# Attention and gated convolution: the attention output of 13 of 16 quads of heads is turned by transposing transfers, and all work is put in a new order

## The chip, the cores and the metric

The kernel runs on one core of a Trainium2 chip. The metric is the device time of one execution in microseconds. Before the change three runs took 176.99, 177.25 and 177.54 us, the median being 177.25 us. The profile shows one further execution, of 176.23 us.

## The reference, cut to what matters

The inputs q, k and v have 8 batches, 8 heads, 576 positions and 64 elements a head. All is float32 in memory and float16 on the matmul engine.

```python
scores = q @ k.T / sqrt(64)                  # for each batch and head, 576 x 576
mask   = (pos_i // 64) >= (pos_j // 64)      # causal in blocks of 64 positions
x      = softmax(where(mask, scores, -1e9)) @ v
x      = x.transpose(0, 2, 1, 3).reshape(8, 576, 512)   # heads side by side
gate   = sigmoid(sum_k conv_w[k] * x[:, t - 4 + k])     # causal, 5 taps a feature
out    = (gate * (x @ w_val)) @ w_out
```

The attention leaves a tile of x with positions on the partitions. The gate's convolution over time and the product with `w_val` both need features on the partitions and positions along the row. So every tile of x is turned once, and the change is about who turns it.

## The kernel before

**Units.** A pair p (0 to 31) is two heads of batch p // 4. A quad Q (0 to 15) is two pairs. A stage n from 0 to 7 is the gated part of batch n on its first 512 positions; the last 64 positions of four batches each are collected in stages 8 and 9.

**One quad.** SyncE loads q and k of four heads (`Lq`, `Lk`, 576 KB each) and v (`Lv`, `Lvt`). VectorE, GpSimd or ScalarE casts them (`cq`, `ck`, `cv`, `cvt`), and VectorE turns q and k (`dq`, `dk`, line 202). TensorE makes the scores in three pieces and a last one (`s.Q.0` to `s.Q.2`, `sl`), ScalarE the exponentials (`e`, `el`, line 242), GpSimd zeroes what the mask hides (`m`), TensorE multiplies with v (`av`, 35 matmuls a head), VectorE divides by the sums (`n`, lines 289 and 290) and writes the tile `x16[p % 4]`, 128 positions x 5 blocks x 128 features of two heads in float16.

**The turn, before.** For every quad TensorE transposes the five 128 x 128 blocks of each of its two pairs against an identity into PSUM (`xtr`, line 298, 10 matmuls a quad). VectorE, for the last two quads ScalarE, copies the two pairs into `xts[b % 2]` (`xt`, line 156). There are two such buffers, one batch each. `xe` copies the last 64 positions aside (`xtl`).

(Each pair has two heads of 64 features, so one block of it has 128 features and the five blocks hold 640 positions, of which 576 are real. A quad's `xtr` covers both pairs: 2 x 5 blocks, and each block is one matmul with its weight load. The profile counts 160 of them for 16 quads.)

**One stage.** TensorE runs the convolution as 80 small matmuls on all of the batch's rows (`cn`, slices of 32 x 32 with the taps on diagonals), ScalarE the tanh (`th`), TensorE `x @ w_val` in four pieces (`val`), VectorE gate times value (`gv`, line 347), TensorE the product with `w_out` in four pieces (`o`), VectorE or ScalarE copies them out of PSUM (`oc`), SyncE stores (`st`, lines 378, 382, 376).

**What sets the order.** One string of words, `PLAN`, is read from left to right; each word issues one of the operations above on the engine behind its `@` (A ScalarE, D VectorE, P GpSimd, S SyncE's queue; a digit is the PSUM bank of a TensorE operation). Each engine runs its own words strictly in that order, and semaphores between engines follow from the data. `w.512` is a matmul on zeros whose result nobody reads. A DMA is issued by SyncE's queue in its place in the string and waits there for its buffer or its data, so all DMAs behind it wait too.

```python
def xtrans(p, cnt, m):                       # before: line 294
    for e in range(2):
        for i in range(5):
            nc.tensor.transpose(out=f16(bk(m, e))[:, 128 * i:128 * i + 128],
                                in_=x16[(p + e) % NX16][0:128, i, 0:2, 0:64], ...)
```

Of the kernel before, what the change touches and what calls it, by code (L numbers as in the profile page):

```python
# [11 lines left out]
wz@D pk@D pp.2@P Lq.0@S Lk.0@A Lk.1@S Lq.1@S cq.0@D dq.0@D id Lcw@S ck.0@D dk.0@D ck.1@P dk.1@D  # L12
w.512@0 w.512@0 w.512@0 w.512@0 w.512@0 w.512@0 w.512@0 w.512@0 w.512@0 w.512@0 w.512@0 w.512@0
w.512@0 w.512@0 w.512@0 s.0.2@02 s.0.1@46 tb cq.1@P fo@D Lv.0.0@S e.0.2@A dq.1@D e.1.2@A p4.0@P
cwc@P s.0.0@02 pv.1@P Lq.2@S e.1.1@A px.0@P cw@6 cT@D Lv.0.3@S cq.2@D e.0.1@A pp.0@P Lv.0.1@S pv.0@P
e.1.0@A w.512@7 w.512@7 sl.0@64 Lvt.0@S el.0.1@A pp.1@P s.1.2@24 cvt.0@D cv.0.3@D el.0.0@A e.0.0@A
e.3.2@A Lv.0.2@S cv.0.2@D s.1.0@60 Lk.2@S cv.0.1@P e.3.0@A dq.2@D e.2.0@A Lwv.1@S Lq.3@S p4.1@P
m.1@P cv.0.0@P av.1@4 m.0@P pp.3@P e.2.2@A s.1.1@06 n.1@D e.2.1@A e.3.1@A Lwv.0@S ck.2@P pp.4@P
av.0@4 dk.2@D s.2.0@02 n.0@D m.2@P av.2@6 m.3@P Lv.1.0@S cq.3@P e.4.0@A DG@D e.5.0@A av.3@4 s.2.2@02
wv.1@A n.2@D wv.0@A xtr.0.2@6 n.3@D e.5.2@A xtr.2.2@4 Lk.3@S e.4.2@A Lk.4@S xt.0.2@D ck.3@P s.2.1@26  # L20
e.4.1@A xt.2.2@D xe.0@P wv.2@P ck.4@P wv.3@D Lv.1.3@S e.5.1@A cn.0@04 m.5@P dk.3@D dq.3@D Lv.1.2@S
Lv.1.1@S th.0.0@A val.0.0@2 cv.1.2@P gv.0.0@D Lvt.1@S val.0.1@3 th.0.1@A Lq.4@S s.3.2@06 Lwo.0@S
val.0.3@2 e.7.2@A gv.0.1@D sl.1@46 dk.4@D gv.0.3@D Lq.5@S cv.1.1@P e.6.2@A cv.1.3@D Lwo.3@S
val.0.2@3 Lvt.2@S gv.0.2@D el.1.0@A cq.4@D px.1@P pp.5@P s.3.0@04 cvt.1@P el.1.1@A e.6.0@A e.7.0@A
Lwo.1@S dq.4@D cv.1.0@P av.5@6 s.3.1@20 n.5@D m.4@P av.4@4 Lv.2.0@S cq.5@D e.7.1@A Lk.5@S e.6.1@A
m.7@P n.4@D m.6@P s.4.0@06 av.7@2 av.6@4 e.8.0@A ck.5@P n.7@D n.6@D e.9.0@A Lk.6@S s.4.1@06 e.8.1@A
Lwo.2@S Lv.2.2@S wo.1@P xtr.4.2@2 Lv.2.3@S Lq.6@S xt.4.2@D wo.0@P e.9.1@A xtr.6.2@4 s.4.2@02 e.8.2@A
xt.6.2@D e.9.2@A m.9@P dq.5@D Lv.2.1@S cn.1@46 val.1.0@0 th.1.0@A dk.5@D xe.1@P gv.1.0@D Lq.7@S
ck.6@P val.1.1@1 s.5.0@24 cq.6@P th.1.1@A e.11.0@A e.10.0@A gv.1.1@D o.0.1@0 oc.0.1@D o.0.2@1
oc.0.2@D cv.2.3@D sl.2@46 el.2.0@A el.2.1@A val.1.2@0 Lvt.3@S cv.2.2@P Lq.8@S s.5.1@24 Lk.7@S  # L30
cvt.2@P Lv.3.2@S e.11.1@A val.1.3@1 m.8@P gv.1.2@D o.0.3@0 dq.6@D dk.6@D s.5.2@46 e.10.1@A cv.2.1@P
Lv.3.3@S e.11.2@A e.10.2@A cv.2.0@P av.8@2 gv.1.3@D n.8@D o.0.0@1 av.9@6 m.11@P s.6.0@24 oc.0.3@D
oc.0.0@A n.9@D av.11@0 st.0.0@S m.10@P cq.8@A e.13.0@A av.10@6 e.12.0@A cq.7@P n.11@D o.1.1@4
cvt.3@P oc.1.1@A n.10@D s.6.1@02 e.13.1@A Lv.3.1@S xtr.8.2@6 xtr.10.2@4 xt.8.2@D Lv.3.0@S xt.10.2@D
e.12.1@A s.6.2@26 dq.7@D cn.2@04 e.12.2@A ck.7@P dk.7@D xe.2@D cv.3.3@P Lk.8@S cv.3.0@P e.13.2@A
m.13@P th.2.0@A o.1.3@2 oc.1.3@D m.12@P dq.8@D th.2.1@A o.1.0@3 sl.3@06 cv.3.1@P el.3.1@A val.2.3@2
cv.3.2@P gv.2.3@D s.7.0@46 oc.1.0@A val.2.2@3 Lvt.4@S Lv.4.3@S o.1.2@2 ck.8@P el.3.0@A e.15.0@A
e.14.0@A gv.2.2@D s.7.2@06 val.2.1@3 e.14.2@A dk.8@D Lq.9@S e.15.2@A Lq.10@S oc.1.2@D Lk.9@S
Lv.4.0@S av.12@4 gv.2.1@D s.7.1@02 n.12@D e.14.1@A Lv.4.1@S val.2.0@6 Lv.4.2@S gv.2.0@D av.13@4
st.0.1@S e.15.1@A s.8.0@06 m.14@P m.15@P av.14@2 n.13@D av.15@4 st.1.0@S ck.9@P Lv.5.3@S e.16.0@A  # L40
e.17.0@A n.14@D n.15@D o.2.1@0 oc.2.1@D Lv.5.2@S s.8.2@26 Lk.10@S e.16.2@A xtr.14.2@4 xtr.12.2@0
Lk.11@S xt.14.2@D e.17.2@A cq.10@P o.2.0@2 oc.2.0@A s.8.1@46 xt.12.2@D e.16.1@A e.17.1@A cn.3@02
cq.9@P cv.4.3@D val.3.1@4 val.3.2@5 Lvt.5@S dk.9@D xe.3@P Lv.5.1@S dq.9@D th.3.0@A gv.3.1@D th.3.1@A
s.9.0@06 e.18.0@A gv.3.2@D val.3.0@4 gv.3.0@D cvt.5@D e.19.0@A o.2.2@5 Lq.11@S oc.2.2@D sl.4@02
cv.4.0@P dq.10@D o.2.3@4 el.4.0@A cvt.4@P cv.4.1@P Lv.6.3@S s.9.1@06 el.4.1@A e.18.1@A oc.2.3@D
m.16@P Lk.12@S cv.4.2@P st.1.1@S e.19.1@A ck.10@D av.16@2 n.16@D cn.8@40 val.8.0@6 th.8.1@A th.8.0@A
# [24 lines left out]
gv.7.1@D val.9.0@1 val.7.3@5 cn.9@26 th.9.0@A gv.9.0@D val.9.1@0 th.9.1@A val.7.2@2 gv.9.1@D
oc.6.0@A val.7.0@1 gv.7.2@D o.9.0@0 o.9.1@4 gv.7.0@D st.6.1@S gv.7.3@D oc.9.1@A st.6.0@S o.7.0@1
oc.9.0@D o.7.1@0 o.7.2@2 oc.7.0@A o.7.3@1 oc.7.1@D st.9.0@S st.7.0@S oc.7.2@D oc.7.3@AD st.7.1@SA
# [4 lines left out]
def kernel(  # L78
# [12 lines left out]
    fp16 = mybir.dt.float16  # L91
# [3 lines left out]
    B, H, SEQ, D = q.shape  # L95
# [14 lines left out]
    def ring(n, shape, dt, tag):  # L110
        return [const(shape, dt, f"{tag}_{i}") for i in range(n)]
# [23 lines left out]
    xts = ring(NX, [128, 4, 644], fp16, "xt")  # L135
# [8 lines left out]
    slot = {}  # L144
# [4 lines left out]
    def two(s):  # L149
        return PS[0:128, s:s + 2]  # L150

    def f16(ap):
        return ap.bitcast(fp16)

    def copy(eng, o, i):
        (eng.copy if eng is nc.scalar else eng.tensor_copy)(out=o, in_=i)  # L156
# [279 lines left out]
    def pads_x(i, m):  # L436
        m.memset(xts[i][0:128, 0:4, 0:4], 0.0)
# [47 lines left out]
```

## Time and profile before

| what | value |
|---|---|
| median of three runs | 177.25 us |
| the profiled execution | 176.23 us, of which the span of the engines is 174.4 us |
| mean granted TensorE clock | 0.971 of full speed |
| TensorE busy | 161.7 us, 93% of the span |
| VectorE, ScalarE, GpSimd busy | 129.9, 131.5, 69.2 us |
| first convolution matmul, last matmul of all | starts at 28.41 us, ends at about 170.15 us |
| moved by DMA | 40.30 MB, mean 231 GB/s |

The span runs from the first instruction to the last event of the core; 1.83 us of the execution lie outside it. Three stretches have different limits: the head up to the first convolution (loads, casts, the first exponentials), the long middle, and the 4.25 us behind the last matmul (copy out, store, its landing). The page gives shares for the whole span, so the stretches have to be asked for one by one.

### The profile page before, as it was taken

Reading aid. Unit: us, or ns where it says so; the run is one execution under the profiler, and the core shown is the slowest. Engines: PE = TensorE matmul, PEld = TensorE weight load, DVE = VectorE, ACT = ScalarE, POOL = GpSimd, SP = SyncE. Lnnn points to the kernel's source line nnn. Section 1 sums busy time; section 2 is a strip of 40 time slices with the busy share of each in tenths; the row PEclk is TensorE's granted clock in tenths of the full one; section 3 lists DMA queues with packets and bytes.
Section 4 is the critical chain, followed back from the end, with each engine's and each line's share of the span. In section 5 each row is a group of like instructions: output and inputs, shape, how many; then the busy total and the mean of one; then the engine's idle time right before and its main releaser. Section 6 shows DMA issues by size and latency. Waiting matters only on the chain.

```text
span 174.4 us, 6916 instructions
## 1 busy us (share of the span) xinstructions
PE 161.7 (93%) x3013; PEld 94.8 (54%) x3013; DVE 129.9 (74%) x202; ACT 131.5 (75%) x160; POOL 69.2 (40%) x141
## 2 busy tenths in 40 slices
PE   7448999989999999999999999999999999999990
PEld 2123677367445673576366854675437563855640
DVE  1599399998878887879697798779899836741650
ACT  3039999987969899767979799899879698456320
POOL 1284565954595817085505134433603022210000
PEclk9985599999999999999999999999999999999999
DMA  5999997999799699999997596999320005403246
GB/s 176 397 323 296 381 327 195 312 264 301 194 336 271 187 325 334 277 296 319 343 337 242 114 402 198 305 233 357 136 79 2 4 4 194 172 4 120 81 163 241
DMA packets 48216, 40.30 MB, mean 231 GB/s; under 512 B 38453, under 2 KB 38453, under 8 KB 48186
## 3 DMA queue, kind: packets, MB, share of 16 engines
q1 hardware_dynamic: 47898, 39.01, 72.8%
q10 hardware_dynamic: 288, 0.85, 1.4%
q8 instruction: 23, 0.38, 0.9%
q14 instruction: 7, 0.06, 0.1%
HBM read 30.42 MB, written 9.44 MB: 228 GB/s over the span
## 4 chain that ended last, share of the span: by engine, by line
PE 70%; DVE 12%; ACT 7%; issue 5%; DMA 3%; ACTq 0%; DVEq 0%
PE PS L99 65%; ACT pt L242 6%; PE PS L298 5%; DMA qks<-in_q_dram 3%; DVE x L290 3%; DVE qk L156 2%; DVE kT L202 2%; DVE gv L347 2%; DVE qT L202 1%; DVE osb L156 1%; DVE rc L289 1%; ACT osb L156 1%; DVE xt L156 0%; DVE v16t L156 0%; ACT v L156 0%
## 5 line engine op out<-in xcount | busy, mean ns | idle before, releaser
L242 ACT ACTIVATE pt<-PS 128x1024 f16<-128x1024 f32 (+1 forms) x112 | 97.8, 937 | 23.3 <-PE PS L99 20.9
L99 PE MATMUL PS<-qT,kT 32*128 32x64 f16 (+4 forms) x768 | 37.6, 291 | 5.7 <-DVE kT L202 4.5
L99 PEld LDWEIGHTS <-pt 128*128 128x128 f16 x960 | 32.0, 99 | 7.1 <-issue 3.1
L99 PE MATMUL PS<-w_out,gv 128*128 128x512 f16 x144 | 35.3, 380 | 0.1
L347 DVE SCALAR_TENSOR_TENSOR gv<-th,PS 128x512 f16<-128x512 f32 x36 | 24.0, 681 | 14.6 <-ACT th L332 9.3
L156 POOL CAST qk<-qks 128x1152 f16<-128x1152 f32 x22 | 25.3, 1165 | 21.4 <-DVE kT L202 12.3
L99 PE MATMUL PS<-v,pt 128*128 128x65 f16 x896 | 33.0, 195 | 0.9 <-ACT pt L242 0.7
L99 PE MATMUL PS<-xt,w_val 128*128 128x512 f16 x128 | 31.9, 381 | 0.0
L99 PEld LDWEIGHTS <-kT 32*128 32x128 f16 x768 | 16.2, 95 | 28.2 <-issue 16.7
L263 POOL MEMSET pt<- 64x384 f16 x32 | 13.8, 430 | 37.8 <-ACT pt L242 37.1
L290 DVE TENSOR_TENSOR x<-PS,rc 128x640 f16<-128x640 f32 x32 | 26.4, 824 | 1.1
L99 PEld LDWEIGHTS <-w_val 128*128 128x128 f16 x160 | 13.7, 98 | 14.6 <-issue 3.8
L99 PEld LDWEIGHTS <-gv 128*128 128x128 f16 x144 | 12.8, 98 | 14.4 <-issue 0.9
L202 DVE STREAM_TRANSPOSE qT<-qk 128x576 f32<-128x576 f32 x16 | 19.9, 1243 | 0.1
L202 DVE STREAM_TRANSPOSE kT<-qk 128x576 f32<-128x576 f32 x16 | 19.7, 1243 | 0.0
L332 ACT ACTIVATE th<-PS 128x1024 f32<-128x1024 f32 (+1 forms) x20 | 17.7, 947 | 2.2 <-PE PS L99 2.2
L156 DVE COPY osb<-PS 128x512 f32<-128x512 f32 (+1 forms) x20 | 13.4, 671 | 7.3 <-PE PS L99 5.8
L156 ACT COPY osb<-PS 128x512 f32<-128x512 f32 (+1 forms) x17 | 9.7, 583 | 9.0 <-PE PS L99 8.3
L289 DVE RECIPROCAL rc<-PS 128x10 f32<-128x10 f32 x32 | 6.8, 212 | 8.4 <-PE PS L99 5.7
L156 DVE COPY xt<-PS 128x1152 f16<-128x1152 f16 x14 | 10.2, 754 | 3.8 <-PE PS L298 3.7
L156 POOL COPY xtl<-xt 128x272 f16<-128x272 f16 x7 | 3.9, 551 | 22.0 <-DVE xt L156 16.7
L156 POOL CAST v<-vst 128x512 f16<-128x512 f32 x18 | 11.4, 642 | 3.0 <-DMA vst<-in_v_dram 2.4
(45 smaller groups left out, 113.8 us busy)
## 6 DMA issues: line engine op xcount, KB each, us to landing
qks<-in_q_dram SPq DMA_DIRECT2D x16, 576.0 KB, 7.0
qks<-in_k_dram SPq DMA_DIRECT2D x15, 576.0 KB, 7.0
vst<-in_v_dram SPq DMA_DIRECT2D x32, 256.0 KB, 6.4
out_dram<-osb SPq DMA_DIRECT2D x15, 512.0 KB, 4.3
out_dram<-osb SPq DMA_DIRECT2D x5, 256.0 KB, 2.5
vtst<-in_v_dram SPq DMA_DIRECT2D x8, 128.0 KB, 5.4
th<-in_moe_w_val_dram SPq DMA_DIRECT2D x2, 512.0 KB, 8.9
w_st<-in_moe_w_out_dram SPq DMA_DIRECT2D x4, 256.0 KB, 8.7
```

Source lines behind the costliest of these rows:

```text
L99: nc.tensor.matmul(out=out, lhsT=lhsT, rhs=rhs, start=start, stop=stop, skip_group_check=True)
L156: (eng.copy if eng is nc.scalar else eng.tensor_copy)(out=o, in_=i)
L202: m.transpose(out=o.bitcast(fp32)[..., 0], in_=qk16[(2 * Q + i) % NQ16][0:128].bitcast(fp32))
L242: nc.scalar.activation(out=o, in_=i, func=AF.Exp, bias=0.0, scale=0.125)
L263: m.memset(pt[64:128, 0:2, 0:1536].rearrange("p h (t s) -> p h t s", t=3)[:, :, :, 0:64], 0.0)
L289: nc.vector.reciprocal(out=rc, in_=O[:, :, :, 64:65])
L290: nc.vector.tensor_tensor(out=x16[p % NX16][0:128].rearrange("p i h d -> p h i d"), in0=O[:, :, :, 0:64], in1=rc.to_broadcast([128, 2, 5, ...
L298: nc.tensor.transpose(out=f16(bk(m, e))[:, 128 * i:128 * i + 128], in_=x16[(p + e) % NX16][0:128, i, 0:2, 0:64], identity=ident16[0:128, 0 ...
L332: nc.scalar.activation(out=ths[turn(n) % NTH][0:128, 2 * s:2 * s + 2, 0:width(n)], in_=two(slot["cn", n][s])[:, :, 0:width(n)], func=AF.Ta ...
L347: nc.vector.scalar_tensor_tensor(out=gvs[turn(n) % NGV][0:128, e * x:e * x + e, 0:w], in0=ths[turn(n) % NTH][0:128, e * x:e * x + e, 0:w], ...
```

## The change

Quads 0 and 1 and the last, 15, keep the turn on TensorE (`xtr.0.2`, `xtr.2.2`, `xtr.30.2`). For the other 13 quads, pairs 4 to 29, there is a new operation `xd` (line 307): a transposing DMA for each pair, 26 in all, which reads the 128 x 640 float16 tile `x16` (164 KB) and writes it turned into `xts`. All of them are issued by SyncE's queue, among the loads and stores. Row starts in `xts` are moved from column 4 to column 16, the row grows from 644 to 656 elements, and the readers (`xin`, `ends_x`, `pads_x`) follow; the columns beyond 592 receive the 64 positions that are not real and are read by nobody.

The string `PLAN` is written anew as a whole. Counted by words: `w` goes from 17 to 32 (30 of 512 columns, 2 of 256), all before the first convolution; `xt` on VectorE from 14 to 3 and on ScalarE from 2 to none; copies out of PSUM (`oc`) on ScalarE from 16 to 22 and on VectorE from 19 to 14, and one that was split over both engines goes to ScalarE whole; casts of k on VectorE from 3 to 8 and on GpSimd from 13 to 8. The first load of k moves from ScalarE's queue to SyncE's, behind the first load of q. All other operations are there in the same number.

```diff
-wz@D pk@D pp.2@P Lq.0@S Lk.0@A Lk.1@S Lq.1@S cq.0@D dq.0@D id Lcw@S ck.0@D dk.0@D ck.1@P dk.1@D
...
+wz@D Lq.0@S pk@D pp.1@P pv.0@P cq.0@D id pp.2@P dq.0@D Lk.0@S ck.0@D Lcw@S cwc@P px.0@P dk.0@D
...
-    xts = ring(NX, [128, 4, 644], fp16, "xt")
+    xts = ring(NX, [128, 4, 656], fp16, "xt")
...
-        copy(m, xts[(p // 4) % NX][0:128, p % 4:p % 4 + 2, 4:580], f16(two(slot["xtr", p]))[:, :, 0:576])
+        copy(m, xts[(p // 4) % NX][0:128, p % 4:p % 4 + 2, 16:592], f16(two(slot["xtr", p]))[:, :, 0:576])
+
+    def dma_x(p, m):
+        m.dma_start_transpose(out=xts[(p // 4) % NX][0:128, p % 4, 16:656].rearrange("p (i s) -> p i s", s=128),
+                              in_=x16[p % NX16][0:128].rearrange("p i h d -> p (i h d)"))
...
-        copy(m, xtl[b // 4][0:128, 0:4, pr, 0:68, o], xts[b % NX][0:128, 0:4, 512:580])
+        copy(m, xtl[b // 4][0:128, 0:4, pr, 0:68, o], xts[b % NX][0:128, 0:4, 524:592])
...
-            return xts[n % NX][r, g, kk:kk + 512]
+            return xts[n % NX][r, g, 12 + kk:524 + kk]
...
-        "xe": ends_x, "cn": conv, "th": gate, "val": val, ...
+        "xe": ends_x, "xd": dma_x, "cn": conv, "th": gate, "val": val, ...
```

Three places show how instructions moved. The first is TensorE from the last `av` of batch 2 to its convolution. `v` and `v16t` are the values, `pt` the exponentials, `w_out` marks a piece of an earlier batch's output, `qT`,`kT` a piece of scores, `xt`,`DG` the convolution; weight loads and repeats are left out. Before:

```order
L99 MATMUL PS<-v16t_100,pt_0_108 128x65
L99 MATMUL PS<-w_out,gv_124 128x512
L99 MATMUL PS<-qT_92,kT_95 128x448
L99 MATMUL PS<-qT_92,kT_95 128x64
L298 MATMUL PS<-ident_63,x_0_113 128x128
L298 MATMUL PS<-ident_63,x_3_116 128x128
L99 MATMUL PS<-qT_92,kT_95 128x320
L99 MATMUL PS<-qT_92,kT_95 128x192
L99 MATMUL PS<-xt_117,DG 32x512
```

And in the change:

```order
L100 MATMUL PS<-v16t_100,pt_0_108 128x65
L100 MATMUL PS<-qT_92,kT_95 128x448
L100 MATMUL PS<-qT_92,kT_95 128x64
L100 MATMUL PS<-w_out,gv_124 128x512
L100 MATMUL PS<-qT_92,kT_95 128x320
L100 MATMUL PS<-qT_92,kT_95 128x192
L100 MATMUL PS<-xt_117,DG 32x512
```

The transposes of pairs 8 to 11 are gone from TensorE; two pieces of scores and three pieces of output (the piece behind the last scores is two pieces in a row) stand between the last `av` and the convolution.

The second place is SyncE's queue around the same batch, in the change. `qks` and `vst` are loads of q, k and v; `xt_117` is the buffer that the convolution of batch 2 reads:

```order
L162 DMA qks_75<-in_k_dram 128x1152
L162 DMA qks_76<-in_q_dram 128x1152
L162 DMA qks_74<-in_q_dram 128x1152
L162 DMA qks_77<-in_k_dram 128x1152
L307 DMA_TRANSPOSE xt_117<-x_0_113 128x5x128
L307 DMA_TRANSPOSE xt_117<-x_1_114 128x5x128
L307 DMA_TRANSPOSE xt_117<-x_2_115 128x5x128
L307 DMA_TRANSPOSE xt_117<-x_3_116 128x5x128
L172 DMA vst_85<-in_v_dram 128x8x64
```

Four transposing transfers stand in one row behind four loads, and the loads of v for the next quads stand behind them.

The third is the start of VectorE, whose first rows are the same in both up to the turn of k of quad 0; then the change has

```order
L157 CAST qk_0_88<-qks_72 128x1152
L203 STREAM_TRANSPOSE qT_92<-qk_0_88 128x18x32
L157 CAST qk_1_89<-qks_73 128x1152
L203 STREAM_TRANSPOSE kT_95<-qk_1_89 128x18x32
L157 CAST convT<-PS 128x20
L157 COPY idfold<-ident_63 32x32 x4
L203 STREAM_TRANSPOSE qT_93<-qk_2_90 128x18x32
L203 STREAM_TRANSPOSE kT_96<-qk_3_91 128x18x32
```

where before the turn of k of quad 1 came straight after that of quad 0. What changed ahead of these rows is the queue: q and k of quad 0 were issued at the same time on two queues, and now stand one behind the other on SyncE's.

More of the change, by code (lines that the diff above doesn't have):

```diff
@@ L17 @@
[L17 to L22, printed above, removed]
@@ new lines @@
+s.1.2@04 Lv.1.0@S Lwv.0@S e.2.0@A e.2.2@A e.3.1@A m.2@P cv.0.2@D av.1@2 Lwv.1@S av.0@0 ck.2@D dk.2@D
+n.1@D n.0@D av.2@6 e.3.2@A m.3@P w.512@4 w.512@4 w.512@4 w.512@4 s.2.2@42 e.5.2@A n.2@D av.3@0
+Lq.3@S e.4.2@A n.3@D s.2.1@26 e.4.1@A xtr.0.2@4 xtr.2.2@0 xt.0.2@D wv.3@P Lk.3@S Lv.1.3@S wv.0@P
+e.5.1@A w.512@2 s.2.0@24 xt.2.2@D wv.2@A e.4.0@A wv.1@P cq.3@P cn.0@06 Lq.4@S ck.3@D Lv.1.1@S
+Lvt.1@S cq.4@P dk.3@D val.0.3@2 e.5.0@A m.5@P Lv.1.2@S th.0.1@A dq.3@D gv.0.3@D Lk.4@S m.4@P
+val.0.1@3 s.3.0@46 th.0.0@A e.6.0@A val.0.2@2 Lwo.0@S sl.1@04 e.7.0@A gv.0.1@D el.1.0@A cv.1.0@P
@@ new lines @@
+gv.1.0@D m.8@P e.10.1@A val.1.2@1 dq.6@D sl.2@46 th.1.1@A el.2.1@A el.2.0@A gv.1.2@D val.1.3@0
+Lv.2.0@S s.5.2@26 cv.2.1@P cvt.2@P val.1.1@1 gv.1.3@D cv.2.2@P e.11.2@A s.5.0@46 e.10.2@A ck.6@D
+Lv.3.1@S cv.2.0@P e.10.0@A m.10@P gv.1.1@D Lk.7@S av.8@0 e.11.0@A av.9@2 m.11@P dk.6@D n.8@D
+cv.3.1@A n.9@D av.10@4 Lq.8@S n.10@D s.6.0@06 e.12.0@A Lq.7@S Lk.8@S av.11@2 n.11@D s.6.1@40 xd.8@S
+e.13.0@A xd.9@S cq.7@P ck.8@P ck.7@D e.13.1@A o.1.1@6 xd.10@S s.6.2@02 xd.11@S o.1.0@7 e.12.1@A
+e.12.2@A Lv.3.3@S oc.1.1@D o.1.3@6 dq.7@D xe.2@P dk.7@D oc.1.0@D e.13.2@A Lv.3.2@S m.13@P cq.8@P
@@ new lines @@
+oc.1.3@A cn.2@04 th.2.0@A th.2.1@A val.2.2@6 sl.3@20 cv.3.3@P dk.8@D dq.8@D m.12@P Lv.3.0@S
+val.2.1@7 el.3.0@A Lvt.3@S el.3.1@A s.7.2@24 cv.3.0@P gv.2.2@D val.2.3@6 gv.2.1@D cvt.3@D cv.3.2@A
+e.15.2@A xe.1@P gv.2.3@D e.14.2@A av.12@0 n.12@D s.7.0@46 av.13@2 e.15.0@A s.7.1@06 e.14.0@A
+e.14.1@A Lq.9@S e.15.1@A st.0.1@S n.13@D cq.9@P dq.9@D s.8.0@42 e.17.0@A e.16.0@A Lq.10@S val.2.0@0
+Lk.9@S m.14@P gv.2.0@D av.14@6 m.15@P av.15@2 n.14@D s.8.2@04 e.16.2@A Lvt.4@S o.1.2@6 n.15@D
+Lv.4.0@S o.2.0@7 xd.13@S e.17.2@A ck.9@D oc.1.2@A dk.9@D st.0.0@S oc.2.0@A s.8.1@02 e.17.1@A cq.10@P
@@ L74 @@
+gv.7.0@D gv.7.3@D oc.9.0@A gv.7.1@D o.7.1@2 o.7.0@3 o.7.3@5 st.6.0@S oc.9.1@A oc.7.0@D st.9.0@S
+o.7.2@4 oc.7.1@A oc.7.2@A oc.7.3@A st.7.0@S st.7.1@SA
 """
@@ L443 @@
         "sl": scores_last, "el": exps_last, "m": mask, "av": av, "n": norm, "xtr": xtrans, "xt": evac_x,
-        "xe": ends_x, "cn": conv, "th": gate, "val": val, "gv": gated, "o": proj, "oc": evac_out, "st": store, "cwc": cast_taps, "cw": taps,
+        "xe": ends_x, "xd": dma_x, "cn": conv, "th": gate, "val": val, "gv": gated, "o": proj, "oc": evac_out, "st": store, "cwc": cast_taps, "cw": taps,
         "cT": evac_taps, "DG": diags, "w": warm, "wz": zeros, "tb": table, "id": ident, "fo": fold,
```

99 lines of the change are left out of this document (43 added, 56 removed).

## The prediction

> **What bounds the kernel now.** I read the busy times of the page first, then the same by stretch, then the chain of waits, last the groups and the DMA view. In a stretch the columns are length, then busy time of TensorE, its weight loads, VectorE, ScalarE and GpSimd, granted clock, DMA share and GB/s.
>
> ```profile
> 28.41:170.15 141.74, 140.31 (x2717) 82.77 (x2716) 110.33 (x169) 113.02 (x137) 55.64 (x105) 1.00 0.71 216
> ```
>
> From the first convolution to the last matmul TensorE works 140.3 of 141.7 us at full clock. VectorE and ScalarE have some 30 us to spare there. So in the middle one microsecond taken from TensorE is one microsecond of time, and one taken from another engine is nothing, as long as TensorE never waits. The head is different:
>
> ```profile
> 0.74 5.46 DMA qks<-in_q_dram
> ...
> 6.23 0.77 DVE qk L156
> ...
> 7.03 1.26 DVE qT L202
> ...
> 9.44 1.27 DVE kT L202
> ...
> 11.44 6.15 ACT pt L242 x8
> ...
> 18.68 3.07 PE PS L99 x44
> ```
>
> In this chain of waits the first loads, VectorE's casts and turns of quad 0, and then ScalarE's exponentials end last. TensorE is no limit there.
>
> **Term 1, the transposes.** The group and a piece of the chain:
>
> ```profile
> L298 PE MATMUL PS<-ident,x 128*128 128x128 f16 x160 | 11.1, 219 | 0.2 <-issue 0.2
> ...
> L156 DVE COPY xt<-PS 128x1152 f16<-128x1152 f16 x14 | 10.2, 754 | 3.8 <-PE PS L298 3.7
> ```
> ```profile
> 78.96 1.22 PE PS L298 x20
> ```
>
> A transpose lasts 219 ns, but they overlap, and 20 (two quads in a row) take 1.22 us of the chain, 61 ns each. 13 quads of 10 leave: 130 x 61 ns = 7.9 us, all of it behind 28.41 us and before the end. The eleven copies that leave VectorE (11 x 754 ns = 8.3 us) and the two that leave ScalarE are work of engines with spare time: 0. So are the shifted casts and copies out.
>
> **Term 2, the head.** Both first loads were under way together. The windows of DMA traffic, last column GB/s, tell what q alone would need:
>
> ```profile
> 0.00:2.00 2.00, 0.77 (x2) 0.28 (x3) 0.55 (x5) 0.82 (x1) 0.85 (x7) 1.00 0.16 32
> 2.00:3.00 1.00, 1.00 (x4) 0.39 (x3) 0.00 (x0) 0.67 (x2) 0.00 (x0) 1.00 0.84 166
> 3.00:4.00 1.00, 1.00 (x4) 0.36 (x3) 0.00 (x0) 0.00 (x0) 0.00 (x0) 1.00 1.00 396
> 4.00:5.00 1.00, 1.00 (x4) 0.35 (x3) 0.00 (x0) 0.00 (x0) 0.00 (x0) 1.00 1.04 415
> ```
>
> 0.06 + 0.17 + 0.40 MB have moved by 4.0 us, and q is 0.59 MB; q and k together (1.18 MB) by about 5.4 us, and the cast began 0.85 us later, at 6.23. With k behind it, q should land at about 4.8, and cast and turn of q are done before k is there at 6.2. The chain of quad 0 then ends 1.4 us earlier (lower bound 0, if the two loads still share the engines). The exponentials follow in an unbroken row: av of pair 3, the last before the first convolution, waits for the fourteenth of them in both orders (counted in the two strings), so the first convolution also comes 1.4 us earlier. The 15 more matmuls on zeros stand where TensorE waits for ScalarE; they cost 0, and if that cover is gone 15 x 0.21 = 3.2 us (the first ones below ran 15 in 5.01 us, half of it at half clock). They may keep the clock up:
>
> ```profile
> 1.23 5.01 PE L99 MATMUL PS<-wz 128*128 128x512 f16 x15 [1.23 <-DVE wz L408]
> ...
> 10.75 1.42 PE L99 MATMUL PS<-qT,kT 32*128 32x320 f16 x32 [4.51 <-DVE kT L202]
> ```
> ```profile
> 10.00:20.00 10.00, 8.32 (x111) 3.92 (x112) 7.46 (x13) 8.41 (x11) 7.15 (x22) 0.57 1.05 318
> ```
>
> After an idle of 4.5 us the clock fell to half for about ten. ScalarE was busy 8.4 us of that window, so a full clock is worth 0 there, at most half of the 3.07 us of TensorE in the chain, 1.5 us.
>
> **Term 3, the tail.** The last copy was split over two engines; now two whole ones follow each other on ScalarE, 2 x 0.59 against 0.91 us: +0.3.
>
> ```profile
> 167.60 0.59 ACT L156 COPY osb<-PS 128x512 f32<-128x512 f32 x1 [0.28 <-PE PS L99]
> ...
> 170.23 0.37 ACT L156 COPY osb<-PS 128x256 f32<-128x256 f32 x1 [2.05 <-PE PS L99]
> 170.64 0.42 DVE L156 COPY osb<-PS 128x256 f32<-128x256 f32 x1 [0.62 <-ACT osb L156]
> ```
>
> **Term 4, the new wait.** The convolution of batch b needs all four transfers of the batch. TensorE's queue is in order: if they have not landed, it and everything behind it stand still. What lies between the last av and the convolution is the cover. Its prices are start to start:
>
> ```profile
> 58.69 0.89 PE L99 MATMUL PS<-v,pt 128*128 128x65 f16 x24
> ...
> 59.60 1.03 PE L99 MATMUL PS<-w_out,gv 128*128 128x512 f16 x4
> 60.56 0.63 PE L99 MATMUL PS<-qT,kT 32*128 32x448 f16 x16
> 61.12 1.29 PE L298 MATMUL PS<-ident,x 128*128 128x128 f16 x20
> ...
> 64.63 1.90 PE L99 MATMUL PS<-w_out,gv 128*128 128x512 f16 x8
> 66.46 0.30 PE L99 MATMUL PS<-qT,kT 32*128 32x64 f16 x16
> 66.69 0.61 PE L99 MATMUL PS<-xt,w_val 128*128 128x512 f16 x2
> ```
> ```profile
> L290 DVE TENSOR_TENSOR x<-PS,rc 128x640 f16<-128x640 f32 x32 | 26.4, 824 | 1.1
> ...
> L289 DVE RECIPROCAL rc<-PS 128x10 f32<-128x10 f32 x32 | 6.8, 212 | 8.4 <-PE PS L99 5.7 <-ACT pt L242 2.5
> ```
>
> A piece of scores is 0.56 us, a piece of output 0.92, a last piece of scores 0.23, an av 0.91. Batch 1 has 2 scores and 4 outputs, 4.8 us; batch 2 has 2 and 3, 3.9; batch 3 has 2, a last one and 5, 6.0; batch 4 has 2, 2 and a value piece (taken like an output), 3.9; batch 5 has 2 and 5, 5.7; batch 6 has 3 and 4, 5.4. VectorE's normalization goes off first (212 + 824 ns, with handovers 1.1 us), which leaves 3.7, 2.8, 4.9, 2.8, 4.6 and 4.3 us from the issue of the last transfer to its landing. Batch 7's transfers (pairs 28 and 29) come two av before the last and are covered.
>
> No row shows a transposing transfer. The nearest by size and by direction, in the stages 30:60, 60:90, 90:116 and 116:150 us (last column: median us from issue to landing):
>
> ```profile
> vtst<-in_v_dram SPq DMA_DIRECT2D x2, 128.0 KB, 7.3
> out_dram<-osb SPq DMA_DIRECT2D x1, 512.0 KB, 3.6
> ...
> vtst<-in_v_dram SPq DMA_DIRECT2D x2, 128.0 KB, 4.6
> out_dram<-osb SPq DMA_DIRECT2D x4, 512.0 KB, 5.7
> ...
> vtst<-in_v_dram SPq DMA_DIRECT2D x2, 128.0 KB, 6.2
> out_dram<-osb SPq DMA_DIRECT2D x3, 512.0 KB, 5.3
> ...
> out_dram<-osb SPq DMA_DIRECT2D x5, 512.0 KB, 3.8
> ...
> DMA to landing us min/median/max: 2.2/3.6/6.4
> ```
>
> A store also reads the core's own memory, but has 0.36 MB more, 0.9 us at the 400 GB/s above. Batch 1 falls into the first of these stages, 2 and 3 into the second, 4 and 5 into the third, 6 into the last. Less 0.9, stores give 2.7, 4.8, 4.4 and 2.9 us, and waits of 2.0 (batch 2) + 1.6 (batch 4) = 3.6 us. The small loads give 3.6 + 1.8 + 3.4 + 1.6 = 10.4 us in batches 1, 2, 4 and 5. With the shortest landing of a store, 2.2 us (last row), it is 0. I take 5, nearer to the stores: nothing has to come from outside the core, yet SyncE sends four in a row behind loads.
>
> The queue itself: 26 issues at the 0.4 us that a plain one takes are 10 us of SyncE, which has room, but a transfer that waits for its normalization holds the loads behind it. And the engines are not idle:
>
> ```profile
> 60.00:70.00 10.00, 10.00 (x179) 5.08 (x177) 8.17 (x13) 8.94 (x12) 4.43 (x9) 1.00 1.06 320
> ```
> ```profile
> 0.74 0.39 SPq L161 DMA_DIRECT2D qks<-in_q_dram  x1
> ```
>
> 26 x 164 KB add 4.3 MB to 40.3, most of it in a stretch whose DMA share is at 1 already. That is why I don't take less than the stores.
>
> **Sum.** 174.4 - 7.9 - 1.4 + 0.3 + 5 = 170.4 us of span; with the 1.83 us around it 172.2, against 176.23 of the profiled execution. The runs' median lies 1.0 above that execution, so 173.
>
> The Trainium skill speaks against this change: VectorE: DVE Perf Modes, section The three transpose paths, gives a 128 x 128 block 390 ns on TensorE and 1309 ns by DMA, and its table of rules prefers TensorE where PSUM will do. The trace has 219 ns, 61 on the chain; the DMA figure no row shows. Five blocks in turn would be an estimated 6.5 us a transfer, 170 us for 26: far slower. DMA: Bandwidth & Descriptors, section Latency and other measured facts, has 261 GB/s for transposing, an estimated 0.6 us each, 16 us in all, which would leave the sum as it is.
>
> **The rivals.**
>
> *Nothing waits.* Landing stays below 2.8 us. For it: stores land in 2.2 us where the queue is empty. Against: batches 2 and 4 lie in full stretches. 165.4 of span, 168.2 us.
>
> *They queue like small loads.* For it: the DMA share of 1. Against: they read on the chip. 10.4 instead of 5: 178.6 us. At 9 us of waits the gain is just spent.
>
> *They go one after another.* This is the slow side. If the four of a batch don't overlap, and each takes the 2.4 us of the lightest store below, the last lands 9.6 us after the first is ready. The first is ready three av, 2.8 us, before the last, so its effective landing is 6.8 us. Waits 3.1 + 4.0 + 1.9 + 4.0 + 2.2 + 2.5 = 17.7 us, 183.1 of span, 186 us. It decides from an effective landing of about 5.4 us. For it: SyncE issues them in one row. Against: plain DMAs overlap freely. A single wait over 4.5 us could also drop the clock, as in the head. The block figure of the Trainium skill's VectorE: DVE Perf Modes, The three transpose paths, would fit this case.
>
> ```profile
> out_dram<-osb SPq DMA_DIRECT2D x3, 256.0 KB, 2.4
> ```
>
> **How the numbers follow.** Forecast 0.43 (170 to 176), nothing waits 0.2, like small loads 0.17, one after another 0.2. No change is within 0.3% (0.5 us), what a measurement here can tell. It lies on the border of the forecast (0.01 of it) and the small loads (0.06): 0.07. Faster is 0.2 + 0.42 = 0.62, slower 0.11 + 0.2 = 0.31. The range reaches from just below "nothing waits", 167.5, into the last case, to 182.
>
> **What would show it.** Right: no transposes between the first convolution and pair 30, the first scores at about 9.3 us, the first convolution at about 27, waits of TensorE on `xt` before convolutions 2 and 4 of 1 to 3 us each. Wrong: landings of `xt` over 5.4 us, long waits at every convolution, half clock behind one of them, casts that wait for loads after 60 us, or the first convolution later than 28.4.

## The result and the profile after

The change makes the kernel slower: 186.36 us (median of 4 runs, 183.78 to 187.3) against 177.12 before, a ratio of 1.044 with a 95% interval of 1.032 to 1.056. The forecast of 173 was wrong in sign. The four runs fall into two faster ones (183.78 and 186.16 us) and two slower ones (186.55, which is the profiled one, and 187.3); medians here are of all runs of a kernel, every ratio of its faster runs alone.

The page of the change, busy times and the main DMA queue (packets, MB, share of 16 engines' span):

```profile
span 184.5 us, 6734 instructions
...
PE 162.0 (88%) x2898; PEld 89.5 (48%) x2898; DVE 122.7 (67%) x188; ACT 129.4 (70%) x161; POOL 68.7 (37%) x140
...
q1 hardware_dynamic: 65514, 43.86, 91.1%
...
PE 54%; DMA 14%; ACT 12%; DVE 10%; SPq 5%; issue 3%; POOL 1%; ACTq 0%; DVEq 0%; POOLq 0%
```

The last line is the chain of waits by engine. Before it was

```profile
PE 70%; DVE 12%; ACT 7%; issue 5%; DMA 3%; ACTq 0%; DVEq 0%
```

with 3% of DMA and nothing of SyncE's queue (SPq); now 19% of the chain are the two. From the first convolution to the last matmul of the change, columns as in the prediction:

```profile
28.02:180.10 152.08, 139.35 (x2586) 77.48 (x2585) 102.86 (x154) 110.75 (x138) 52.33 (x102) 0.99 0.92 230
```

The middle takes 152.08 us where it took 141.74. TensorE is busy 1.0 us less and idle 12.7 us where it was 1.4. The head is 0.4 us shorter, the 4.4 us behind the last matmul 0.15 longer. So the whole loss lies in the middle. What TensorE and GpSimd wait for there (total, times, longest):

```profile
PE PS L100 <- DMA xt<-x: 5.7, 6, 2.3
...
PEld L100 <- DMA xt<-x: 4.5, 3, 3.1
...
POOL v L157 <- DMA vst<-in_v_dram: 23.0, 9, 6.3
```

TensorE and its weight loads (PEld; their waits overlap TensorE's and do not add to them) now wait for turned tiles. The casts of v wait 23.0 us for their loads; before it was 2.4:

```profile
POOL v L156 <- DMA vst<-in_v_dram: 2.4, 1, 2.4
```

And the new transfers themselves, on SyncE's queue (ns min/median/max of the issue) and to their landing:

```profile
L307 SPq DMA_TRANSPOSE xt<-x x26: 1201/1294/3037, 40.0 to 163.5; - x26
...
DMA to landing us min/median/max: 2.6/4.4/7.6
```

One issue holds the queue for 1.2 to 3.0 us, where a plain load takes 0.4. How this reaches TensorE is seen best at batch 5. The time lines of SyncE's queue, of VectorE (the last normalization of the batch) and of TensorE (its convolution):

```profile
121.20 1.32 SPq L162 DMA_DIRECT2D qks<-in_q_dram  x1
122.62 4.15 SPq L307 DMA_TRANSPOSE xt<-x  x3
126.83 2.75 SPq L172 DMA_DIRECT2D vst<-in_v_dram  x2
```
```profile
121.90 0.82 DVE L291 TENSOR_TENSOR x<-PS,rc 128x640 f16<-128x640 f32 x1
```
```profile
127.47 0.39 PE L100 MATMUL PS<-xt,DG 32*32 32x512 f16 x1
130.17 0.82 PE L100 MATMUL PS<-xt,DG 32*32 32x512 f16 x2 [2.32 <-DMA xt<-x]
131.18 1.84 PE L100 MATMUL PS<-xt,DG 32*32 32x512 f16 x77 [0.18 <-DMA xt<-x]
```

The last tile is ready at 122.72. Its transfer is issued by 126.77, behind two others of the same batch, and lands 4.4 us later. The convolution starts in earnest 8.5 us after the normalization. Batches 2, 3 and 4 have 4.0, 6.6 and 5.4 us in the same way.

### The profile page after: what moved, and what is told of

Read it like the earlier page. It is cut to its first block, busy times and chain, and to the rows that moved or that the text cites. A ratio compares the mean times of both kernels' runs of the same rounds, so it can differ in the third digit from the quotient of the medians.

```text
span 184.5 us, 6734 instructions
## 1 busy us (share of the span) xinstructions
PE 162.0 (88%) x2898; PEld 89.5 (48%) x2898; DVE 122.7 (67%) x188; ACT 129.4 (70%) x161; POOL 68.7 (37%) x140
## 3 DMA queue, kind: packets, MB, share of 16 engines
q1 hardware_dynamic: 65514, 43.86, 91.1%
## 4 chain that ended last, share of the span: by engine, by line
PE 54%; DMA 14%; ACT 12%; DVE 10%; SPq 5%; issue 3%; POOL 1%; ACTq 0%; DVEq 0%; POOLq 0%
PE PS L100 54%; ACT pt L243 10%; DMA xt<-x 6%; DMA vst<-in_v_dram 6%; DMA qks<-in_q_dram 2%; SPq L307 2%; DVE qT L203 2%; DVE qk L157 2%; DVE kT L203 2%; DVE x L291 2%; SPq L162 1%; SPq L172 1%; DVE v L157 1%; DVE xt L157 1%; PE PS L299 1%
## 5 line engine op out<-in xcount | busy, mean ns | idle before, releaser
L100 PE MATMUL PS<-qT,kT 32*128 32x64 f16 (+4 forms) x768 | 37.1, 284 | 5.7 <-DVE convT L157 2.2
L100 PEld LDWEIGHTS <-pt 128*128 128x128 f16 x960 | 31.2, 98 | 8.3 <-issue 6.2
L100 PE MATMUL PS<-v,pt 128*128 128x65 f16 x896 | 32.2, 194 | 2.8 <-POOL v L157 1.5
L157 POOL CAST qk<-qks 128x1152 f16<-128x1152 f32 x20 | 23.9, 1200 | 20.2 <-DMA qks<-in_q_dram 10.5
L157 ACT COPY osb<-PS 128x512 f32<-128x512 f32 x22 | 12.5, 594 | 12.1 <-PE PS L100 12.1
L100 PE MATMUL PS<-xt,DG 32*32 32x512 f16 x640 | 15.3, 390 | 6.1 <-DMA xt<-x 5.7
L157 DVE COPY osb<-PS 128x512 f32<-128x512 f32 x14 | 9.5, 686 | 12.7 <-PE PS L100 11.4
L100 PEld LDWEIGHTS <-DG 32*32 32x32 f16 x800 | 10.1, 88 | 13.7 <-issue 7.5
L157 DVE CAST qk<-qks 128x1152 f16<-128x1152 f32 x12 | 9.9, 823 | 5.4 <-DMA qks<-in_q_dram 3.5
```

What stands on the lines that cost most here:

```text
L100: nc.tensor.matmul(out=out, lhsT=lhsT, rhs=rhs, start=start, stop=stop, skip_group_check=True)
```

## The experiments

The theories on the loss: transfers hold loads and stores behind them in SyncE's queue (QUEUE in the first runs, then PLACE or HELD); turning keeps the DMA engines busy, so that loads come late (OCCUPATION, ENGINES); the convolution waits for the last transfer's way (WAIT, LANDING); the new order itself is worse (ORDER).

Times of before differ a little from chip to chip (176.7 to 177.5); each ratio is against the runs of before beside it.

### Order and transfers apart

Two kernels undo one half of the change each. `order_pe` has the new order with the 13 quads turned on TensorE again, `xtr` and `xt` put in by hand:

```diff
-xd.4@S ... xd.29@S
+xtr.4.2@0 xt.4.2@D ... xtr.28.2@6 xt.28.2@D
```

> The new order alone: the change's order of work, its head, its loads and stores, but the 13 quads are turned on TensorE again (the transposes put back into free PSUM banks one or two operations ahead of each convolution, their copies on VectorE). Three theories. QUEUE (the transposing transfers hold SyncE's queue and the DMA engines, and loads come late) and WAIT (the convolutions wait for the landing, nothing else) both expect the time of before within about 3 us, 175 to 180 us, since no transfer is left. ORDER (the new order is worse by itself) expects 184 us or more, as the change.

192.09 us, ratio 1.073 (1.067 to 1.080). `swap_in_before` has the order of before with `xd.p@S` right behind each `n.p@D` in place of `xtr` and `xt`:

> The transfers alone: the order of before, where for the 13 quads the transposes and their copies are taken out and a transposing transfer stands behind each normalization. QUEUE and WAIT expect it as slow as the change or slower, 183 us or more (the transposes' 7.9 us are saved here too, but the covers are shorter). ORDER expects the saving to show: 168 to 172 us.

215.56 us, ratio 1.212 (1.205 to 1.219). So neither half stands alone: the transfers in the old order are much worse than in the new one, and the new order with TensorE's transposes put back by hand is slower than the change. The number is what ORDER expected, but it says little about the order itself, since the places of the transposes and their PSUM banks were chosen by hand; the runs below do that better.

### What 26 extra transfers do to the old order

The kernel before stays complete, and 26 extra transfers are added whose result nobody reads, each right behind a normalization's word (four of batch 1 behind a cast of `w_out`). They differ in one thing at a time:

```diff
+m.dma_start_transpose(out=spare, in_=x16)           # idle_turning
+m.dma_start(out=spare, in_=x16)                     # idle_plain, 164 KB
+m.dma_start(out=spare[:, 0:16], in_=x16[:, 0:16])   # idle_tiny, 4 KB
+m.dma_start_transpose(out=spare, in_=w_val_sb)      # idle_const: waits for nothing
```

> The kernel before, complete, plus 26 transposing transfers at the places where pairs 4 to 29 are normalized; they read the same tiles and write to a spare place that nobody reads, so no convolution waits for one. QUEUE expects it slower than before by 5 us or more (182 to 190 us), with casts that wait for loads. WAIT expects before within 1 us (176 to 178.5 us).

> As idle_turning, but the 26 transfers copy the same 164 KB without turning them. If the harm of QUEUE is the rate at which a transfer turns (100 GB/s in the trace of the change), this is within 2 us of before, 176 to 179 us. If it is the bytes, or the wait for the normalization ahead of the loads, it is as slow as idle_turning.

> The kernel before, complete, with 26 unread plain copies of 16 columns of x16 (4 KB each) issued by SyncE's queue right behind each normalization's word, pairs 4 to 29. They add next to no bytes, but each waits in the queue for its normalization. PLACE: nearly all that the copies of 164 KB cost at these places, so 189 to 194 us. OCCUPATION: 26 x 0.4 us of issue in a queue with room, 177 to 180 us.

> The kernel before, complete, with 26 unread transposing transfers of 164 KB at the same places, but read from the constant weights, so none of them waits for a normalization; they add 26 x 1.6 us of all DMA engines and their time in the queue. PLACE: 178 to 184 us, since nothing waits for data. OCCUPATION: 190 us or more, since loads come 42 us of engine time later.

Measured 206.35 us (ratio 1.163, 1.158 to 1.168), 193.76 (1.090, 1.083 to 1.098), 191.58 (1.071, 1.058 to 1.084) and 195.45 (1.097, 1.083 to 1.110), against 177.06, 177.06, 176.73 and 176.73. So by the ratios 4 KB copies, which do little but wait in SyncE's queue, already cost 7.1%, 12.5 us; the bytes add 1.9%, which the intervals hardly part from nothing, and turning another 7.3%, 13 us. In the last run no transfer waits for data, and it still costs 9.7%, 17 us: that is what OCCUPATION expected, and far above PLACE. The premise behind PLACE was too narrow as well, since a turning transfer holds the queue by its own issue (1.2 to 3.8 us each in this run). So this run doesn't tell a held queue from busy engines. What suffers is seen in the waits of `idle_const` (loads of v late; TensorE behind copies of outputs whose stores are late):

```profile
POOL v L159 <- DMA vst<-in_v_dram: 13.0, 3, 7.6
PE PS L102 <- DVE osb L159: 10.7, 3, 6.3
```

### The change with copies in place of the turning

This is the comparison that settles most. Words, waits, places and sizes of the change stay; only `dma_start_transpose` becomes `dma_start`, of 164 KB or of 4 KB:

```diff
-m.dma_start_transpose(out=xts[...16:656].rearrange("p (i s) -> p i s", s=128), in_=x16[...])
+m.dma_start(out=xts[...16:656], in_=x16[...])              # after_plain
+m.dma_start(out=xts[...16:32], in_=x16[...][:, 0:16])      # after_tiny
```

> The change as it is, but each of its 26 transfers is a plain copy of 16 of the 640 columns (4 KB instead of 164 KB), so the buffers hold old data and the output is not the reference's; one buffer is filled with zeros once at the start by GpSimd. The issues, the places in SyncE's queue, the waits for the normalization and the waits of the convolution all stay; only the bytes and the turning are gone. OCCUPATION (a turning transfer keeps all DMA engines busy some 1.6 us, so loads are late): 168 to 172 us, waits of TensorE on xt small. PLACE (a transfer that waits for its data holds the loads behind it in SyncE's queue): 182 to 188 us as in the change. LANDING (the convolution waits for the last transfer's way through the DMA engines whatever its size): about 2 us after the issue, so some 172 to 176.

> The change as it is, but each of its 26 transfers is a plain copy of the same 164 KB within the core, so what the convolution reads is not turned and the output is not the reference's. OCCUPATION by bytes: 26 x 0.4 us more of the DMA engines than with 4 KB, so 169 to 174 us, well under the change; the turning is then the price, 26 x 1.2 us of the engines more. PLACE: 182 to 188 us as in the change. Rival: the bytes cost as much as the turning, 182 to 188 us, while the copies of 4 KB are fast.

174.30 us (ratio 0.985, 0.974 to 0.996) and 174.97 us (0.987, 0.982 to 0.992). The first lies where LANDING had it, but in neither run does a convolution wait for `xt`, so it isn't by LANDING's mechanism. Copies that wait at the same places for the same data are not slower than before, and PLACE alone doesn't make the loss; what the bytes cost (0.2%) is below what the intervals can tell; and the turning costs all that the change loses: 1.044 - 0.987 is 5.7% or 10 us by the runs, 184.5 - 172.9 = 11.6 us by the spans of the two profiled executions. The transfers of `after_plain`, and its middle:

```profile
L307 SPq DMA_DIRECT2D xt<-x x26: 464/473/2223, 40.5 to 151.4; - x26
...
DMA to landing us min/median/max: 2.1/3.2/5.9
```
```profile
28.52:168.50 139.98, 134.74 (x2586) 76.66 (x2585) 101.92 (x154) 110.74 (x138) 53.11 (x102) 1.00 0.82 249
```

A copy is issued in 0.47 us and lands in 3.2, and no wait of TensorE on `xt` is left. The busy time of the main queue,

```profile
q1 hardware_dynamic: 51786, 43.86, 82.2%
```

is 82.2% of 172.9 us, 142 us, against 91.1% of 184.5, 168 us: for the same 43.86 MB turning takes 26 us more, a good 1.0 us of all 16 engines for each transfer.

### Per issue or per byte

The change with 26 turning transfers of one or three of the five blocks:

```diff
-in_=x16[p % NX16][0:128].rearrange("p i h d -> p (i h d)"))
+in_=x16[p % NX16][0:128].rearrange("p i h d -> p (i h d)")[:, 0:128])   # 0:384
```

> The change with each of its 26 transfers turning only the first of the five blocks of a pair (33 KB instead of 164 KB; the other columns keep old data, the output is not the reference's; one buffer is filled with zeros once by GpSimd). Waits and places stay. PER BYTE (a turning transfer costs the queue and the engines by what it moves): a fifth of the 12 us that lie between turning and copies of 4 KB, 174.3 + 2.4 = 176.7 us; the issue on SyncE's queue well under 1.2 us, the extra engine time 26 x 0.3 us. PER ISSUE (each turning transfer holds the queue for 1.2 us or more whatever its size): 182 to 186 us, with the issue still at 1.2 us.

> As the run before it, with three of the five blocks (98 KB). PER BYTE: three fifths of 12 us, 174.3 + 7.2 = 181.5 us. PER ISSUE: the same as with one block, 182 to 186 us. Rival: a threshold, where TensorE's other work covers the transfers until a size and the time then jumps, so near 175 us with one block and with three.

| blocks turned | median us | ratio (95%) | issue, median ns | landing, median us | main queue busy, us | TensorE's waits on `xt`, us |
|---|---|---|---|---|---|---|
| none, copies of 4 KB | 174.30 | 0.985 (0.974 to 0.996) | 472 | 2.9 | 132 | 0 |
| 1 | 179.27 | 1.010 (1.003 to 1.018) | 1172 | 3.2 | 139 | 1.9 |
| 3 | 184.59 | 1.044 (1.040 to 1.048) | 1212 | 3.8 | 153 | 4.2 |
| 5 | 186.36 | 1.044 (1.032 to 1.056) | 1294 | 4.4 | 168 | 5.7 |

The last four columns are of one profiled execution each; the one with one block took 183.56 us. Neither theory holds alone. The median issue is 1.2 to 1.3 us at any size, and one block already costs 2.5% or 4.5 us of the 10. The engines' time grows with the bytes, some 0.28 us a block, and with it the landing and TensorE's waits on `xt`, while the issue hardly changes. Three blocks cost as much as five within the intervals, so the time isn't linear either.

### Who pays: the convolution or the loads

`after_unread` has copies for the convolution, as `after_plain`, and behind the last copy of each batch the batch's four turning transfers into an unused buffer:

```diff
 xd.8@S ... xd.9@S ... xd.10@S ... xd.11@S
+ex.8@S ex.9@S ex.10@S ex.11@S
```

> The change with plain copies of the 164 KB in place of the turning, as in the run before this one (what the convolution reads is not turned, the output is not the reference's), and the 26 turning transfers as extra work that nobody reads: they read the same tiles, write to a buffer that is no longer in use, and stand in SyncE's queue right behind the last copy of their batch. So the convolution waits for copies alone, and the turning can only hurt the loads behind it. LANDING (the price of the change is the convolution's wait for the last turned tile): 175 to 177 us, as with copies alone, with TensorE's waits on xt gone. OCCUPATION (the price is that loads come late): 184 to 188 us, with GpSimd's casts waiting over 20 us for v.

205.28 us, ratio 1.156 (1.148 to 1.164), far beyond both. A row of its queue, and a wait of its casts:

```profile
69.10 5.81 SPq L314 DMA_TRANSPOSE w_st<-x  x4
```
```profile
POOL v L159 <- DMA vst<-in_v_dram: 41.0, 10, 9.0
```

Four in a row hold the queue for 5.8 us, and the loads behind them come late: the extra transfers cost 30 us against `after_plain`, and TensorE waits 9.2 us on casts of v and only 0.7 on `xt`. So late loads can carry such a loss, whether by the held queue or by the busy engines. It doesn't show that they carry the change's, where a part of the four is sent while the last normalization is still awaited. For that the two kernels with the same words, `after_plain` and the change, can be laid side by side. Each convolution, from its first matmul's start to its last one's end:

| batch | copies, us | turning, us | later at the start | later at the end |
|---|---|---|---|---|
| 1 | 47.30 to 49.51 | 47.85 to 50.08 | 0.55 | 0.57 |
| 2 | 64.99 to 66.34 | 66.66 to 68.68 | 1.67 | 2.34 |
| 3 | 83.55 to 85.25 | 86.48 to 89.73 | 2.93 | 4.48 |
| 4 | 103.08 to 104.43 | 106.60 to 110.40 | 3.52 | 5.97 |
| 5 | 121.16 to 122.51 | 127.47 to 133.02 | 6.31 | 10.51 |
| 6 | 141.26 to 142.82 | 152.89 to 154.45 | 11.63 | 11.63 |

At batch 5, whose rows in the change stand above, `after_plain` has one unbroken row:

```profile
121.16 1.35 PE L100 MATMUL PS<-xt,DG 32*32 32x512 f16 x80
```

The first convolution is 0.5 us earlier in the change, so some 12.1 us are lost up to batch 6. Of these 8.9 arise inside the convolutions of batches 2 to 5, where the waits on `xt` lie, and 3.2 between them, where TensorE waits 1.5 us on casts of v. So in these two executions the convolution pays most of the price, although the casts' own waits for v are longer. What makes the tiles late, the queue or the engines, this doesn't part. `after_vA` was to separate them the other way, with 26 loads of v on ScalarE's queue (`Lv...@S` to `@A`):

> The change, and 26 of its loads of v (those behind the convolution of batch 1) issued by ScalarE's queue in the same places of the order instead of by SyncE's, so that they are no longer held behind turning transfers and don't hold them. HELD (what the turning costs the change is the time that loads and transfers hold each other in one queue): the last transfers of batches 3 to 5 are issued sooner, 178 to 182 us. ENGINES (the cost is the 1.4 us of all DMA engines that each transfer takes): 184 to 187 us as in the change. Rival: ScalarE, now 10 us busier with issues and waiting for buffers, sends its exponentials later: over 188 us.

215.6 us against 177.52: the rival. ScalarE reaches the loads late in its own order, and the casts wait 53.4 us for v. It tells nothing on the other two, which stay open.

### A quiet stretch

Back to the order of before: only quads 12 and 14 turned by transfers, from 135 us and from 151 or 155 us on, where SyncE's queue has only stores left. `late` puts each transfer behind its normalization; `late2` also moves four stores, whose data is ready, ahead of them:

```diff
-n.25@D ... xtr.24.2@0 xt.24.2@D ... xtr.28.2@4 ... xt.28.2@A
+n.25@D xd.25@S ... n.24@D xd.24@S ... n.28@D xd.28@S n.29@D xd.29@S
```
```diff
+st.4.0@S st.4.1@S xd.25@S ... st.5.0@S st.8.0@S xd.28@S
```

> The kernel before with two of its quads, 12 and 14, turned by transfers (4 in all), each issued right behind its normalization, at about 137 and 150 us, where the DMA share is 0.2 to 0.3; 20 transposes and two copies go. The last of quad 12 has some 3.3 us until the convolution of batch 6, quad 14 some 6 us. OCCUPATION and LANDING: with quiet engines a transfer lands in about 3 us, nothing waits long, and 2 x 0.61 = 1.2 us are saved: 175.7 us where before has 176.9. PLACE (a transfer that waits for its data holds what is behind it): only stores stand behind these, so the same. If a turning transfer costs about the same wherever it stands, 10 us / 26 each, it is 1.5 us slower before the gain: 177.2.

> The run before this one with quads 12 and 14 turned by transfers in the old order, and the four stores that stood behind these transfers in SyncE's queue (both of batch 4, the first of batch 5, that of stage 8) now ahead of them; their data is ready before. PLACE (what the four transfers cost was ScalarE's 3.0 us wait for an output buffer whose store was held behind them, and a second one near the end): these waits go, and 10 us of DMA engines more hurt nobody in this stretch: 175.9 us where before has 177.0, 1.2 us saved by 20 transposes less. PRICE (a turning transfer costs some 1 us wherever it stands): 181 us again.

181.59 us (ratio 1.024, 1.019 to 1.030), far above what was expected, and 176.77 (0.998, 0.993 to 1.002). Four stores in another place are worth 4.8 us, 2.7% by the ratios. `late` on SyncE's queue, then on ScalarE:

```profile
135.00 3.68 SPq L306 DMA_TRANSPOSE xt<-x  x2
138.77 10.81 SPq L382 DMA_DIRECT2D out_dram<-osb  x3
```
```profile
142.01 0.58 ACT L156 COPY osb<-PS 128x512 f32<-128x512 f32 x1 [3.02 <-DMA out_dram<-osb]
```

The first held store leaves at 138.77; the copy that needs its buffer waits 3.0 us, the exponentials behind that copy too, and then TensorE, 3.1 us. That is PLACE, shown by one edit. In `late2` the price is gone, but the gain of 1.2 us doesn't show:

```profile
140.57 0.73 PE L298 MATMUL PS<-ident,x 128*128 128x128 f16 x10
141.81 0.97 PE L99 MATMUL PS<-qT,kT 32*128 32x320 f16 x16 [0.51 <-ACT pt L242]
```

Ten transposes less, 0.56 us, and in their place 0.51 us of waiting for exponentials to clear a bank. `late2` can't be told from before (its interval just reaches down to the gain), and no version here is shown to beat it.

### The head

`head` is the kernel before with one word changed (`Lk.0@A` to `Lk.0@S`, behind `Lq.0@S`); `plain_nozero` is `after_plain` without the 17 matmuls on zeros behind the first scores.

> The kernel before with one word changed: k of quad 0 is loaded by SyncE's queue behind q instead of by ScalarE's queue. By the prediction's second term the cast of q starts about 1.3 us earlier (4.9 instead of 6.23), the first scores at 9.3 instead of 10.75, the first convolution 1.4 us earlier, and the time is 1.4 us shorter: 175.5 us where before has 176.9. Rival: what follows the first scores is bound by the loads of the next quads or by the order of scores and values on TensorE, which the word doesn't change, so the first convolution stays within 0.4 us of 28.4 and the time within 0.5 us.

> The change with plain copies in place of the turning (output not the reference's), and without the 17 matmuls on zeros behind the first scores; the 15 ahead of them stay. If the four of them ahead of the scores of quad 2 (22.47 to 23.42 us with ScalarE waiting for TensorE) lie on the path, the first convolution starts about 1.0 us earlier, 27.5 instead of 28.5, and the time is 174.0 us instead of 175.0. If they keep up the clock in the head, it falls to half there, the first convolution comes later than 28.5, and the time is 175.5 to 177 us. If they cost nothing: 175.0.

`head`: 177.14 us, ratio 1.000 (0.996 to 1.003). `plain_nozero`: 174.61 us (0.981, 0.974 to 0.989), which the intervals don't separate from 174.97; its first convolution starts at 28.21 instead of 28.52, at a clock of 0.57 instead of 0.75 from 10 to 20 us. The zeros cost nothing that can be measured. For `head` the convolutions of batches 0, 1 and 2 tell the story, and its chain of waits:

```profile
27.27 1.98 PE L99 MATMUL PS<-xt,DG 32*32 32x512 f16 x80
44.39 1.35 PE L99 MATMUL PS<-xt,DG 32*32 32x512 f16 x80 [0.29 <-DVE xt L156]
63.67 1.40 PE L99 MATMUL PS<-xt,DG 32*32 32x512 f16 x80
```
```profile
16.24 8.98 DMA qks<-in_k_dram
...
37.67 8.41 DMA w_st<-in_moe_w_out_dram
...
53.56 1.18 POOL v L156 x2
54.78 6.78 PE PS L99 x150
```

The first convolution is 1.14 us earlier, as the second term said (28.41 before). At batch 1, 0.17 us are left (44.56), at batch 2 none (63.30). From 16 to 55 us the chain runs over loads and GpSimd's casts, which a faster start doesn't move.

## Why the prediction was wrong, point by point

The forecast was 170.4 us of span, and 184.5 came: 14.1 us more. `after_plain` splits this. Without any wait on transfers the prediction had 165.4; with copies, on which TensorE doesn't wait, it is 172.9. So 7.5 us were a gain that isn't there. The other 6.6 us are the price of turning, forecast at 5 and measured at 11.6 between the two spans (10 by the ratios).

**What bounds the kernel.** The step "one microsecond taken from TensorE is one microsecond of time" failed. It was read from TensorE's 140.3 busy of 141.7 us. In `after_plain` the middle has 134.74 busy, 5.6 us less, but 5.24 idle where there were 1.43, so that of 7.9 us there remain 1.8. TensorE was the busiest engine, and others stood right behind it. Of the new idle time, 3.8 us, most is a wait for ScalarE, which "some 30 us to spare" had ruled out: in this stretch the list of waits has 1.8 us on exponentials, 1.0 on the tanh and 0.5 on a copy out, where before it had 0.5 on exponentials alone. `late2` shows such a wait in one row. Up to 55 us loads and casts stand there too (`head`). The prediction quoted a DMA share at 1 in the same stretch, and used it only for the price of transfers. Why the busy time itself falls by 5.6 and not by 7.9 us stays open.

**Term 1**, the transposes: 130 are gone, and the middle is 1.8 us shorter, not 7.9, even where nothing is turned. That the copies taken from VectorE are worth 0 was not tested by itself.

**Term 2**, the head: the early load gives what was worked out, first scores at 8.91 us (9.3 forecast) and, alone in the old order, 1.14 of 1.4 us at the first convolution. In the change 0.4 arrive there, and in the old order nothing is left at the end. The step that failed is to carry the gain past the loads that follow.

**Term 3**, the tail: +0.3 forecast, 0.15 measured.

**Term 4**, the new wait: right in kind, since convolutions wait for transfers, but at batches 2 to 5 and not at 2 and 4 alone, and wrong in size. The failed step is to price a turning transfer like a plain one: "26 issues at the 0.4 us that a plain one takes", and engines that pay for its bytes alone. The issue takes 1.2 to 3.0 us, in a row with others, and the engines a good 1.0 us more for each than for a copy of the same bytes. So the time from the last normalization to the convolution is 4.0, 6.6, 5.4 and 8.5 us where the cover was 2.8, 4.9, 2.8 and 4.6: waits of 9.4 us in all where 5 were taken. That the same transfers as copies are 10 us faster shows that the turning is the cause; how much of it is the queue and how much the engines is not shown. The landing after an issue, median 4.4 us, lies within the range of the small loads and stores that were taken for it.

**The rivals.** "One after another" gave 186 us, and 186.36 came. Its mechanism is the nearest: the transfers of a batch follow each other in one queue. But the agreement in the number is chance: it had 17.7 us of waits and 9.0 us of gain, and a price of 11.6 and a gain of 1.5 were measured. Its remark on the clock came true behind a shorter wait than the 4.5 us that it named: after the 2.32 us wait of batch 5 the change has a mean clock of 0.83 over ten us. What that costs was not measured.

```profile
130.00:140.00 10.00, 9.58 (x170) 4.46 (x172) 4.45 (x6) 4.54 (x6) 4.26 (x8) 0.83 1.07 338
```

The rule of the Trainium skill that spoke against the change, VectorE: DVE Perf Modes, Rules for kernel authors, prefers TensorE for a 128 x 128 transpose where PSUM will do; it was right in direction, 186.36 us against 177.12. The 1309 ns a block of the Trainium skill's VectorE: DVE Perf Modes, The three transpose paths, would be an estimated 6.5 us a transfer; the trace doesn't agree, its shortest landing of five blocks is 2.6 us. The 261 GB/s of the Trainium skill's DMA: Bandwidth & Descriptors, Latency and other measured facts, by which the sum stayed as it was, are not reached: see the last section.

## What to carry to other kernels

A transfer is priced by three rows, not by its bytes alone: how long its issue holds the queue, what stands behind it in that queue, and how long it keeps the engines. Before work is moved onto a queue, write down which loads and stores will stand behind it, and put those whose data is ready ahead: four stores moved were worth 4.8 us. And where one engine is busy 99% of a stretch, look for the next bound right behind it (banks that wait for another engine, a DMA share near 1) before counting a gain in full; a copy of the same size in place of the disputed operation shows at once how much of the gain is there and what the operation costs.

## What the runs showed of the hardware

A turning transfer on the chip's own memory holds SyncE's queue for at least 1.1 us whatever its size, where a copy of the same bytes takes 0.47. Four in a row held it for 5.3 to 6.9 us (`after_unread` and the change). It moves its bytes far slower than a load: in a quiet stretch of the change with only the last two transfers under way,

```profile
164.00:166.00 2.00, 2.00 (x19) 1.23 (x17) 0.98 (x3) 1.17 (x2) 0.00 (x0) 1.00 0.94 94
```

the engines are busy 94% of the time at 94 GB/s, where loads reach 415 GB/s at a share of 1. Five blocks took 1.4 us of all engines on the mean ((168 - 132) / 26), 164 KB at some 120 GB/s. The two last transfers alone agree: from 162 to 168 us they keep the engines busy 2.8 us, and as copies in `after_plain`, from 150 to 156 us, 1.0 us.
